# Gelu's tanh on up to six W1 items at once: attention, MLP and output projection in one kernel on one core

## The chip, the core and the metric

The kernel runs on one core of one Trainium2 chip. The metric is the device time of one execution in microseconds (us). The engines are named as in the profile: PE multiplies matrices, ACT (ScalarE) applies functions element by element, DVE (VectorE) does the other elementwise work, POOL (GpSimd) a few small things, and SP issues the DMAs.

## What is computed

The input x has 2048 rows of 1024 elements. It is normalized once; the normalized rows feed an attention of 32 heads (head size 32) and an MLP of width 3584, and the two results are multiplied:

```python
xn = _layernorm(x, axis=-1)
s = _A_ref(xn, A_wqkv, A_wo)                       # attention: softmax(q k^T / sqrt(32)) v, then wo
g = _silu(_B_ref(xn, B_w1, B_b1, B_w2, B_b2))
return x + s * g

def _B_ref(x, w1, b1, w2, b2):
    y = _layernorm(x, axis=-1)
    h = _gelu(jnp.einsum("bsd,df->bsf", y, w1) + b1)
    return jnp.einsum("bsf,fd->bsd", h, w2) + b2
```

The gelu is the approximation by tanh: with u = x (1 + 0.044715 x^2), it is x (1 + tanh(0.798 u)) / 2; the factor 1/2 is applied later. All tensors are bf16.

## The kernel before

**Attention.** The 32 heads are taken in eight groups of four. For each group (w in the code, 0 to 7) there are eight query blocks of 256 rows, and for each of those eight key pairs of 256 keys. One such unit (`unit`, L830) has a score matmul on PE (L846), which writes two pairs of PSUM banks, and two exponentials on ACT (L855), each 128 x 1024, which write P tiles in SBUF. Six PSUM banks hold three such pairs, so PE can be at most three exponentials ahead of ACT. PV matmuls (L612) multiply P with V; the row sums of P go through a tree of additions on DVE (`tree`, L877, with L872 and L886) and a matmul with ones. There are 512 units, and so some 1024 exponentials.

**Dense work.** Everything else on PE is called dense: the projections to Q, K and V (L683, L699, recorded at the helper's line 617), the MLP, and at the end the output projection. A dense item takes one of two PSUM banks (6 and 7) and is evicted by DVE.

**MLP.** The rows go through in eight chunks c of 256 rows (NCH = 8). Each chunk has 14 W1 items (NW1 = 14, `w1_item`, L1013): an item computes 256 of the 3584 hidden columns for 256 rows, that is 512 elements per partition, and DVE adds the bias and writes it to slot p % 20 of the ring hT (L1023; p = 14 c + pi, NH = 20 slots). Then four W2 items (`w2_item`, L1045) each read all 14 items of the chunk. A slot of the ring is free for a new W1 item when the four W2 items of its chunk have read it. `seq_mlp` (L1079) sets the order: between the W2 items of chunk c stand the first six W1 items of chunk c + 1, the other eight follow after the fourth.

**Gelu.** It runs in place on groups of neighbouring items in the ring, mostly four (L1027 to L1042): square (L1037), times 0.044715 plus 1 (L1038), times x (L1039), tanh on ACT (L1040), plus 1 (L1041), times x (L1042). The first three and the last two are on DVE. The scratch u is one of two buffers `ut_t[0]` and `ut_t[1]` of 2048 elements per partition, taken in turn (`geg`). In even chunks the groups are 4, 4, 4, 2 items, in odd ones 2, 4, 4, 4, and in the last chunk 2, 4, 4, 2, 2.

**What sets the order.** The kernel does not run loops on the chip: `_Plan` (L33) is a list scheduler in Python that simulates all engines with a cost for each operation (`c_b16`, `c_acts` and so on, L559 to L575), picks for each engine the next operation, and `emit` writes each engine's list with semaphore waits. Dependencies come from tokens such as ("h", slot) and ("ut", buffer). On DVE and ACT `pick` (L149) takes the ready operation with the lowest priority number: evictions and exponentials 0, quotients 1, gelu on DVE 3, trees 3.2, tanh 1. Some that have waited long are raised: DVE operations of priority 3 to 3.5 after 4000 ns, and ACT operations after 2500 ns, which then go ahead of the exponentials. PE takes scores first, as soon as a bank pair is free; a dense chunk is not started when it would leave ACT dry (`guard`). A W2 item is passed over until every DVE operation that its operands depend on has started (L302); PE then takes the head of another dense list. A change of one operation can so reorder everything that comes after it. In one stretch (the third of 30 us) the planner also adds a small pseudo-random term to positions and priorities, computed from the operations' numbers (`nz`, L83).

Of the kernel before, what the change touches and what calls it, by code (L numbers as in the profile page):

```python
# [6 lines left out]
ACT = mybir.ActivationFunctionType  # L7
ALU = mybir.AluOpType
BF16 = mybir.dt.bfloat16
F32 = mybir.dt.float32  # L10
I32 = mybir.dt.int32
# [21 lines left out]
class _Plan:  # L33
# [14 lines left out]
    def add(self, eng, fn, occ, lat, R=(), W=(), prio=3, item=None, sem=None, nbytes=0, rate=180.0, extra=()):  # L48
        o = _Op()
        o.eng, o.fn, o.occ, o.lat, o.prio = eng, fn, occ, lat, prio  # L50
        o.item, o.sem, o.nbytes, o.rate = item, sem, nbytes, rate
        o.idx = len(self.ops)
        o.users, o.ready, o.start, o.fin = [], 0.0, None, None
        o.dead, o.needs_inc, o.count, o.know = False, False, None, None
        o.l2, o.pas, o.exps = None, (), ()
        deps = {}
        for t in R:
            w = self.last_w.get(t)
            if w is not None:
                deps[w] = True  # L60
        for t in W:
            w = self.last_w.get(t)
            if w is not None:
                deps[w] = True
            for r in self.readers.get(t, ()):
                if r is not o:
                    deps.setdefault(r, False)
        for d in extra:
            deps[d] = True
        for t in R:  # L70
            self.readers.setdefault(t, []).append(o)
        for t in W:
            self.last_w[t] = o
            self.readers[t] = []
        deps.pop(o, None)
        o.deps = deps
        o.left = len(deps)
        for d in deps:
            d.users.append(o)
        self.ops.append(o)  # L80
        return o
# [379 lines left out]
def bass_recurrent_scan__mha_block__mixer_channel_mlp__prompt_kernel(  # L461
# [16 lines left out]
    NW1 = FB // 2  # L478
    EPS = 1e-5
    SCALE = 32 ** -0.5  # L480
    GC, GA = 0.7978845608028654, 0.044715
# [11 lines left out]
    with ExitStack() as st:  # L493
        def sb(name, shape, dt):
            return st.enter_context(nc.sbuf_tensor(name, list(shape), dt))
# [2 lines left out]
        o_d = nc.dram_tensor("o_scratch", (HG, 128, S), BF16).ap()  # L498

        NP, NPX, NPA, NH, NW1R, NW2R = 10, 16, 3, 20, 3, 4  # L500
        NTR, NWARM, NG0, AT = 4, 8, 3, 1
        ident = sb("ident", [128, 128], BF16)
        ones = sb("ones", [128, 32], BF16)
# [9 lines left out]
        hT = sb("hT", [128, NH, 2, 256], BF16)  # L513
# [3 lines left out]
        w2r = sb("w2r", [128, NW2R, 7, 256], BF16)  # L517
        b2b = sb("b2b", [128, D], BF16)
        b1T = sb("b1T", [128, FB], BF16)
        ut_t = [sb(f"ut{i}", [128, 4, 512], BF16) for i in range(2)]  # L520
        gw = sb("gw", [128, 4096], BF16)
        z_t = [gw[:, i * 1024:(i + 1) * 1024] for i in range(2)]
        zh_t = gw[:, 2048:4096].bitcast(F32)
# [21 lines left out]
        NXS = 10  # L545
        xst = [h_flat[:, i * 1024:(i + 1) * 1024] for i in range(NXS)]
        xnb = [gw[:, i * 1024:(i + 1) * 1024] for i in range(4)]
        iota_i = ut_t[0][:].rearrange("p a b -> p (a b)")[:, 0:256].bitcast(I32)

        def bank(i, lo=0, hi=512):  # L550
            return ps[:, i * 512 + lo:i * 512 + hi]
# [7 lines left out]
        def c_ps(n):  # L559
            return 77 + 1.0417 * n  # L560
# [4 lines left out]
        def c_b16(n):  # L565
            return 67 + 0.521 * n

        def c_b4(n):
            return 67 + 0.2605 * n
# [4 lines left out]
        def c_acts(n):  # L574
            return 82 + 0.8334 * n  # L575
# [3 lines left out]
        def linked(o, item):  # L579
            d = item.chunks[-1]  # L580
            if d not in o.deps:
                o.left += 1
                d.users.append(o)
            o.deps[d] = True
            item.evacs.append(o)

        def dve(fn, occ, R, W, prio, item=None, extra=()):
            o = add("DVE", fn, occ, DL, R, W, prio, extra=extra)
            if item is not None:
                linked(o, item)  # L590
            return o

        def act(fn, occ, R, W, prio, item=None):
            o = add("ACT", fn, occ, AL, R, W, prio)
            if item is not None:
                linked(o, item)
            return o
# [7 lines left out]
        def chunk(item, fn, occ, R, W=()):  # L605
            o = add("PE", lambda e, fn=fn, item=item: fn(e, item.bank), occ, TL, R, W, item=item)
            item.chunks.append(o)
            return o
# [7 lines left out]
        def mm(e, dst, lhsT, rhs, start, stop):  # L616
            return e.matmul(dst, lhsT=lhsT, rhs=rhs, start=start, stop=stop, skip_group_check=True)  # L617
# [4 lines left out]
        def fl3(t):  # L622
            return t[:].rearrange("p u j q -> p (u j q)")
# [140 lines left out]
        for n in range(NPR):  # L764
            groups = [(2 * n,), (2 * n + 1,)] if n < 2 else [(2 * n, 2 * n + 1)]
            for ts in groups:
                if ts == (AT,):
                    for k, f, sc in ((0, ACT.Copy, 1.0 / D), (1, ACT.Square, D ** -0.5)):
# [6 lines left out]
                                                         op1=ALU.subtract), 65,  # L775
# [209 lines left out]
        nw2, geg = {"n": 0}, {"n": 0}  # L985
# [16 lines left out]
        def make_y(c):  # L1002
            for t2 in range(2):
# [6 lines left out]
                dma(f"yt{t2}", lambda e, t2=t2: e.dma_start_transpose(yT[:, :, t2 * 128:(t2 + 1) * 128], yst_t[t2][:]),  # L1010
                    262144, [("yst", t2)], [("yT", t2)], occ=1300, rate=300.0, lat=2300)

        def w1_item(c, pi):  # L1013
            p = c * NW1 + pi
            gi, hs = p % NW1R, p % NH
            it = _Item("mlp")
            for f2 in range(2):
                for dc in range(DC):
                    def fn(e, b, f2=f2, dc=dc):
                        return mm(e, bank(b, f2 * 256, (f2 + 1) * 256), w1r[:, gi, dc, f2 * 128:f2 * 128 + 128], yT[:, dc, :],  # L1020
                                  dc == 0 and f2 == 0, dc == DC - 1)
                    chunk(it, fn, Q256, [("w1", gi), ("yT", 0), ("yT", 1)])
            w1_ev[p] = dve(lambda e: e.tensor_tensor(hT[:, hs], bank(it.bank).rearrange("p (k t) -> p k t", k=2),  # L1023
                                          b1T[:, 2 * pi:2 * pi + 2].unsqueeze(2).to_broadcast([128, 2, 256]), op=ALU.add),
                c_ps(512), [("b1",)], [("h", hs)], 0, it)
            half = c == NCH - 1 and pi in (NW1 - 3, NW1 - 1)
            if p % 4 != 3 and pi != NW1 - 1 and not (pi == 1 and c % 2) and not half:  # L1027
                return it
            k = 2 if (pi == NW1 - 1 and p % 4 != 3) or (pi == 1 and c % 2) or half else 4
            h0, n = hs - k + 1, k * 512  # L1030
            hs_ = [("h", h0 + i) for i in range(k)]
            ui = geg["n"] % 2
            geg["n"] += 1
            x_ = hT[:, h0:h0 + k].rearrange("p s k t -> p (s k t)")
            u_ = ut_t[ui][:].rearrange("p a b -> p (a b)")[:, 0:n]
            gp, ga = (1.4, -1) if c == NCH - 1 and pi >= 5 else (3, 1)
            dve(lambda e: e.tensor_tensor(u_, x_, x_, op=ALU.mult), c_b16(n), hs_, [("ut", ui)], gp)  # L1037
            dve(lambda e: e.tensor_scalar(u_, u_, GA, 1.0, op0=ALU.mult, op1=ALU.add), c_b4(n), [("ut", ui)], [("ut", ui)], gp)  # L1038
            dve(lambda e: e.tensor_tensor(u_, u_, x_, op=ALU.mult), c_b16(n), [("ut", ui)] + hs_, [("ut", ui)], gp)  # L1039
            act(lambda e: e.activation(u_, u_, ACT.Tanh, scale=GC), c_acts(n), [("ut", ui)], [("ut", ui)], ga)  # L1040
            dve(lambda e: e.tensor_scalar_add(u_, u_, 1.0), c_b4(n), [("ut", ui)], [("ut", ui)], gp)  # L1041
            dve(lambda e: e.tensor_tensor(x_, u_, x_, op=ALU.mult), c_b16(n), [("ut", ui)] + hs_, hs_, gp)  # L1042
            return it

        def w2_item(c, q):  # L1045
# [54 lines left out]
        def mlp(u0, u1):  # L1100
            seq = list(seq_mlp())
            cost = {"y": 0.0, "w1": 1.74, "w2": 6.1}
            total = sum(cost[s_[0]] for s_ in seq)
            at = 0.0
            for s_ in seq:
                pos = u0 + (u1 - u0) * at / total
                at += cost[s_[0]]
                if s_[0] == "y":
                    make_y(s_[1])
                    continue  # L1110
                if s_[0] == "w1":
                    load_w1(s_[1] * NW1 + s_[2])
                    it = w1_item(s_[1], s_[2])
                else:
                    for r in range(4):
                        w2slot[(s_[1], s_[2], r)] = load_w2(s_[2], r, [w1_ev[(4, 6, 8, 10)[r]]] if s_[1] + s_[2] == 0 else ())
                    it = w2_item(s_[1], s_[2])
                it.pos = pos
                (mq if s_[0] == "w1" else plan.dense["w2"]).append(it)
# [134 lines left out]
        for w in range(HG):  # L1254
# [24 lines left out]
            for qb in range(NQB):  # L1279
# [44 lines left out]
                for t2 in range(2):  # L1324
# [16 lines left out]
                    for nh in range(2):  # L1341
# [38 lines left out]
                        if fin and i2 == 3:  # L1380
                            hs_ = fl3(PR[0])[:, i2 * 512:(i2 + 1) * 512]
# [84 lines left out]
```

## Time and profile before

| | |
|---|---|
| median of 3 runs | 1036.16 us (1034.75 to 1036.66) |
| profiled execution | 1036.81 us |
| its span, first to last instruction | 1035.0 us |
| busy: ACT, PE, DVE | 98%, 96%, 92% |
| exponentials (L855) | 988 in the largest group, 923.6 us |
| tanh of gelu (L1040) | 33: 23 of 2048, 10 of 1024 elements per partition |
| dense MLP matmuls | 1792 for W1 (228.2 us busy), 1792 for W2 (223.7 us) |

The profile gives each group of instructions with its line, engine, operation, output and inputs, shape, number, busy time, mean duration, and the idle time of the engine before it with what ended it. Durations on one engine can overlap, so the mean duration is not the engine's time for one. The timeline gives starts and lengths in us; the table of stages gives, for a stretch, the busy time of PE, PE's weight loads, DVE, ACT and POOL, then PE's granted clock, the DMA share and GB/s. The granted clock was 0.997 over the span.

### The profile page before, as it was taken

Reading aid. Unit: us, or ns where it says so; the run is one execution under the profiler, and the core shown is the slowest. Engines: PE = TensorE matmul, PEld = TensorE weight load, DVE = VectorE, ACT = ScalarE, POOL = GpSimd, SP = SyncE. Lnnn points to the kernel's source line nnn. Section 1 sums busy time; section 2 is a strip of 40 time slices with the busy share of each in tenths; the row PEclk is TensorE's granted clock in tenths of the full one; section 3 lists DMA queues with packets and bytes.
Section 4 is the critical chain, followed back from the end, with each engine's and each line's share of the span. In section 5 each row is a group of like instructions: output and inputs, shape, how many; then the busy total and the mean of one; then the engine's idle time right before and its main releaser. Section 6 shows DMA issues by size and latency. Waiting matters only on the chain.

```text
span 1035.0 us, 31625 instructions
## 1 busy us (share of the span) xinstructions
PE 994.5 (96%) x14148; PEld 633.3 (61%) x14217; DVE 955.7 (92%) x1343; ACT 1015.9 (98%) x1093; POOL 12.2 (1%) x21
## 2 busy tenths in 40 slices
PE   8999999999999999999999999999999999999996
PEld 6656566666766566666665666666656665654433
DVE  7899999899799999997899999998999889978896
ACT  7999999999999999999999999999999999999996
POOL 2200000000000000000000000000000000000000
PEclk9999999999999999999999999999999999999998
DMA  7967756545766657446457575565365762963321
GB/s 204 171 155 212 192 151 188 166 114 153 205 182 143 177 163 221 120 133 190 136 147 196 149 224 164 149 181 160 84 165 161 208 177 70 294 209 121 121 84 53
DMA packets 318199, 167.99 MB, mean 162 GB/s; under 512 B 56688, under 2 KB 306032, under 8 KB 318064
## 3 DMA queue, kind: packets, MB, share of 16 engines
q1 hardware_dynamic: 318064, 165.98, 58.1%
q8 instruction: 111, 1.82, 0.7%
q14 instruction: 24, 0.20, 0.1%
HBM read 146.55 MB, written 12.06 MB: 153 GB/s over the span
## 4 chain that ended last, share of the span: by engine, by line
ACT 84%; PE 9%; DMA 3%; DVE 2%; issue 0%; SPq 0%; POOL 0%; DVEq 0%; another core or an unknown queue 0%
ACT P L855 78%; PE ps L617 6%; ACT ut L1040 4%; DMA w2r<-in_B_w_dram 2%; PE ps L846 2%; PE ps L612 1%; ACT gw L1067 1%; ACT P L1157 1%; DVE stats L785 1%; DMA xnT<-gw 0%; DMA hT<-in_A_x_dram 0%; DVE gw L748 0%; DVE PA L872 0%; DVE hT L1391 0%; ACT w2r L855 0%
## 5 line engine op out<-in xcount | busy, mean ns | idle before, releaser
L855 ACT ACTIVATE P<-ps 128x1024 bf16<-128x1024 f32 x988 | 923.6, 1238 | 2.9 <-PE ps L846 2.8
L872 DVE TENSOR_TENSOR PA<-P 128x2048 bf16<-128x2048 bf16 x173 | 209.5, 1215 | 33.5 <-ACT P L855 32.4
L617 PE MATMUL ps<-yT,w1r 128*128 128x256 bf16 x1792 | 228.2, 273 | 0.8 <-DVE QKT L702 0.5
L617 PE MATMUL ps<-w2r,hT 128*128 128x256 bf16 x1792 | 223.7, 273 | 4.0 <-DMA w2r<-in_B_w_dram 2.6
L846 PE MATMUL ps<-QKT 32*128 32x256 bf16 x4032 | 200.2, 273 | 12.9 <-ACT P L855 9.3
L886 DVE TENSOR_TENSOR PR<-PR,PA 128x2048 bf16<-128x2048 bf16 x173 | 209.4, 1211 | 1.3
L617 PEld LDWEIGHTS ps<-yT,w1r 128*128 128x128 bf16 x1792 | 163.6, 98 | 54.8 <-issue 30.2
L617 PEld LDWEIGHTS ps<-w2r,hT 128*128 128x128 bf16 x1792 | 163.3, 98 | 54.6 <-issue 30.8
L846 PEld LDWEIGHTS ps<-QKT 32*128 32x128 bf16 x4032 | 59.8, 92 | 142.1 <-ACT P L855 135.3
L612 PE MATMUL ps<-P,V 128*32 128x256 bf16 (+1 forms) x4080 | 136.8, 272 | 0.3 <-issue 0.3
L617 PE MATMUL ps<-xnT,wqk 128*128 128x512 bf16 (+1 forms) x507 | 118.7, 360 | 7.2 <-issue 2.0
L612 PEld LDWEIGHTS ps<-P,V 128*32 128x32 bf16 x4080 | 95.8, 96 | 31.3 <-issue 22.5
L617 PE MATMUL ps<-wv,xnT 128*128 128x256 bf16 (+1 forms) x575 | 85.8, 285 | 0.9 <-DVE QKT L702 0.7
L617 PEld LDWEIGHTS ps<-xnT,wqk 128*128 128x128 bf16 x560 | 49.3, 98 | 53.7 <-issue 15.6
L1023 DVE TENSOR_TENSOR hT<-ps,b1T 128x512 bf16<-128x512 f32 x112 | 76.4, 682 | 1.8 <-PE ps L617 1.1
L872 DVE TENSOR_TENSOR PR<-P 128x2048 bf16<-128x2048 bf16 x60 | 72.6, 1210 | 1.0 <-ACT P L855 0.8
L617 PEld LDWEIGHTS ps<-wv,xnT 128*128 128x128 bf16 x576 | 53.0, 98 | 22.2 <-issue 9.3
L1040 ACT ACTIVATE ut<-ut 128x2048 bf16<-128x2048 bf16 (+1 forms) x33 | 62.1, 1883 | 0.0
L941 DVE STREAM_TRANSPOSE nt<-ps 128x256 f32<-128x256 f32 x63 | 27.8, 442 | 14.9 <-PE ps L612 14.8
L702 DVE CAST QKT<-ps 128x512 bf16<-128x512 f32 x58 | 39.6, 683 | 1.8 <-PE ps L617 1.4
L1037 DVE TENSOR_TENSOR ut<-hT 128x2048 bf16<-128x2048 bf16 (+1 forms) x33 | 34.7, 1052 | 0.1
L1042 DVE TENSOR_TENSOR hT<-ut,hT 128x2048 bf16<-128x2048 bf16 (+1 forms) x33 | 34.6, 1050 | 0.0
(107 smaller groups left out, 581.3 us busy)
## 6 DMA issues: line engine op xcount, KB each, us to landing
w1r<-in_B_w_dram SPq DMA_DIRECT2D x112, 512.0 KB, 4.5
w2r<-in_B_w_dram SPq DMA_DIRECT2D x128, 448.0 KB, 4.6
hT<-in_A_x_dram SPq DMA_DIRECT2D x20, 256.0 KB, 3.8
wqk<-in_A_wqkv_dram SPq DMA_DIRECT2D x16, 256.0 KB, 4.3
yst<-in_A_x_dram SPq DMA_DIRECT2D x16, 256.0 KB, 4.7
g_scratch<-gw SPq DMA_DIRECT2D x32, 128.0 KB, 3.8
o_scratch<-ot SPq DMA_DIRECT2D x56, 64.0 KB, 3.6
xnT<-o_scratch SPq DMA_DIRECT2D x7, 512.0 KB, 7.2
```

What stands on the lines that cost most here:

```text
L612: ins = e.matmul(dst(j), lhsT=lhsT(j), rhs=rhs(j), start=start, stop=stop, tile_position=(0, 32 * j), skip_group_check=True)
L617: return e.matmul(dst, lhsT=lhsT, rhs=rhs, start=start, stop=stop, skip_group_check=True)
L702: dve(lambda e: e.tensor_copy(QKT[sl][:, which, tq * 512:(tq + 1) * 512], bank(it.bank)), c_ps(512), [], [(nm, sl, 2 * tq), (nm, sl, 2 * t ...
L846: ins = e.matmul(bank(b0[j], kk * 256, (kk + 1) * 256), lhsT=QKT[sl][32 * j:32 * j + 32, 1, kb * 128:(kb + 1) * 128], rhs=QKT[sl][32 * j:3 ...
L855: x = act(lambda e, h=h: e.activation(Pt[pi][:, 2 * h:2 * h + 2].rearrange("p j k q -> p (j k q)"), ps[:, pr[h] * 1024:(pr[h] + 1) * 1024] ...
L872: return dve(lambda e: e.tensor_tensor(dst[:].rearrange("p u j q -> p (u j) q"), src[:].rearrange("p u j k q -> p (u j) k q")[:, :, 0, :], ...
L886: return dve(lambda e: e.tensor_tensor(fl3(pr), fl3(pr), fl3(PA[i]), op=ALU.add), c_b16(2048), [("PA", i), tok], [tok], 3.2)
L941: dve(lambda e: e.transpose(nt_t[:], bank(pv.bank, 256, 512)), c_ps(256) + 120, [], [("nt",)], prio, pv)
L1023: w1_ev[p] = dve(lambda e: e.tensor_tensor(hT[:, hs], bank(it.bank).rearrange("p (k t) -> p k t", k=2), b1T[:, 2 * pi:2 * pi + 2].unsqueez ...
L1037: dve(lambda e: e.tensor_tensor(u_, x_, x_, op=ALU.mult), c_b16(n), hs_, [("ut", ui)], gp)
L1040: act(lambda e: e.activation(u_, u_, ACT.Tanh, scale=GC), c_acts(n), [("ut", ui)], [("ut", ui)], ga)
L1042: dve(lambda e: e.tensor_tensor(x_, u_, x_, op=ALU.mult), c_b16(n), [("ut", ui)] + hs_, hs_, gp)
```

## The change

The two scratch buffers become one tensor of eight items' width, with `ut_t[0]` and `ut_t[1]` as its halves. A table GRUNS, made ahead, says at which item a run ends and how long it is: up to six items (GMAX = 6), not across a chunk's end and not across the end of the ring; in the last chunk at most four, and two near its end. The DVE steps of a run are done in parts of at most four items, each part with its own half of the scratch tensor; a run of more than four starts with half 0 and puts the rest in half 1. One tanh then runs over all of the run's elements at once, up to 3072 per partition; it reads and writes both halves. Priorities and planner costs are as before.

```diff
+        GMAX = 6
-        ut_t = [sb(f"ut{i}", [128, 4, 512], BF16) for i in range(2)]
+        utw = sb("ut", [128, 8, 512], BF16)
+        ut_t = [utw[:, 4 * i:4 * i + 4] for i in range(2)]
...
+        GRUNS = {}
+        for c_ in range(NCH):
+            p_, end = c_ * NW1, (c_ + 1) * NW1
+            while p_ < end:
+                k_ = min(GMAX, end - p_, NH - p_ % NH)
+                if c_ == NCH - 1:
+                    k_ = min(k_, 2 if end - p_ <= 4 else 4)
+                GRUNS[p_ + k_ - 1] = k_
+                p_ += k_
...
-            half = c == NCH - 1 and pi in (NW1 - 3, NW1 - 1)
-            if p % 4 != 3 and pi != NW1 - 1 and not (pi == 1 and c % 2) and not half:
+            run = GRUNS.get(p)
+            if run is None:
                 return it
-            k = 2 if (pi == NW1 - 1 and p % 4 != 3) or (pi == 1 and c % 2) or half else 4
-            h0, n = hs - k + 1, k * 512
-            ui = geg["n"] % 2
-            geg["n"] += 1
+            hh = hs - run + 1
...
+            for h0 in range(hh, hh + run, 4):
+                k = min(4, hh + run - h0)
+                ui = 0 if h0 > hh or run > 4 else geg["n"] % 2
+                parts.append([h0, k, ui])
+            if run > 4:
+                parts[1][2] = 1
+                geg["n"] = 0
+            else:
+                geg["n"] += 1
...
+            for h0, k, ui in parts:
+                hs_ = [("h", h0 + i) for i in range(k)]
...
+                dve(lambda e, u_=u_, x_=x_: e.tensor_tensor(u_, x_, x_, op=ALU.mult), c_b16(n), hs_, [("ut", ui)], gp)
...
+            u0 = 4 * parts[0][2]
+            ua = utw[:, u0:u0 + run].rearrange("p a b -> p (a b)")
+            uts = [("ut", q_[2]) for q_ in parts]
+            act(lambda e: e.activation(ua, ua, ACT.Tanh, scale=GC), c_acts(run * 512), uts, uts, ga)
+            for x_, u_, n, hs_, ui in views:
+                dve(lambda e, u_=u_: e.tensor_scalar_add(u_, u_, 1.0), c_b4(n), [("ut", ui)], [("ut", ui)], gp)
+                dve(lambda e, u_=u_, x_=x_: e.tensor_tensor(x_, u_, x_, op=ALU.mult), c_b16(n), [("ut", ui)] + hs_, hs_, gp)
             return it
```

More of the change, by code (lines that the diff above doesn't have):

```diff
@@ L547, in bass_recurrent_scan__mha_block__mixer_channel_mlp__prompt_kernel @@
         xnb = [gw[:, i * 1024:(i + 1) * 1024] for i in range(4)]
-        iota_i = ut_t[0][:].rearrange("p a b -> p (a b)")[:, 0:256].bitcast(I32)
+        iota_i = utw[:].rearrange("p a b -> p (a b)")[:, 0:256].bitcast(I32)
         def bank(i, lo=0, hi=512):
@@ L1025, in w1_item @@
                 c_ps(512), [("b1",)], [("h", hs)], 0, it)
-            half = c == NCH - 1 and pi in (NW1 - 3, NW1 - 1)
-            if p % 4 != 3 and pi != NW1 - 1 and not (pi == 1 and c % 2) and not half:
-                return it
-            k = 2 if (pi == NW1 - 1 and p % 4 != 3) or (pi == 1 and c % 2) or half else 4
-            h0, n = hs - k + 1, k * 512
-            hs_ = [("h", h0 + i) for i in range(k)]
-            ui = geg["n"] % 2
-            geg["n"] += 1
-            x_ = hT[:, h0:h0 + k].rearrange("p s k t -> p (s k t)")
@@ L1035, in w1_item @@
-            u_ = ut_t[ui][:].rearrange("p a b -> p (a b)")[:, 0:n]
-            gp, ga = (1.4, -1) if c == NCH - 1 and pi >= 5 else (3, 1)
[L1037 to L1040, printed above, removed]
@@ L1041, in w1_item @@
-            dve(lambda e: e.tensor_scalar_add(u_, u_, 1.0), c_b4(n), [("ut", ui)], [("ut", ui)], gp)
-            dve(lambda e: e.tensor_tensor(x_, u_, x_, op=ALU.mult), c_b16(n), [("ut", ui)] + hs_, hs_, gp)
+            run = GRUNS.get(p)
+            if run is None:
+                return it
+            hh = hs - run + 1
+            gp, ga = (1.4, -1) if c == NCH - 1 and pi >= 5 else (3, 1)
+            parts = []
+            for h0 in range(hh, hh + run, 4):
+                k = min(4, hh + run - h0)
+                ui = 0 if h0 > hh or run > 4 else geg["n"] % 2
+                parts.append([h0, k, ui])
@@ new lines, in w1_item @@
+            if run > 4:
[3 more added lines that the diff above has]
+                geg["n"] += 1
+            views = []
+            for h0, k, ui in parts:
+                hs_ = [("h", h0 + i) for i in range(k)]
+                n = k * 512
+                x_ = hT[:, h0:h0 + k].rearrange("p s k t -> p (s k t)")
+                u_ = utw[:, 4 * ui:4 * ui + k].rearrange("p a b -> p (a b)")
+                views.append((x_, u_, n, hs_, ui))
+                dve(lambda e, u_=u_, x_=x_: e.tensor_tensor(u_, x_, x_, op=ALU.mult), c_b16(n), hs_, [("ut", ui)], gp)
+                dve(lambda e, u_=u_: e.tensor_scalar(u_, u_, GA, 1.0, op0=ALU.mult, op1=ALU.add), c_b4(n), [("ut", ui)], [("ut", ui)], gp)
+                dve(lambda e, u_=u_, x_=x_: e.tensor_tensor(u_, u_, x_, op=ALU.mult), c_b16(n), [("ut", ui)] + hs_, [("ut", ui)], gp)
```

## The prediction

> **What bounds the kernel now.** I read the page first: busy time, then the chain that ended last, then ScalarE's own groups with shapes kept apart.
>
> ```profile
> PE 994.5 (96%) x14148; PEld 633.3 (61%) x14217; DVE 955.7 (92%) x1343; ACT 1015.9 (98%) x1093; POOL 12.2 (1%) x21
> ...
> ACT 84%; PE 9%; DMA 3%; DVE 2%; issue 0%; SPq 0%; POOL 0%; DVEq 0%; another core or an unknown queue 0%
> ...
> L855 ACT ACTIVATE P<-ps 128x1024 bf16<-128x1024 f32 x988 | 923.6, 1238 | 2.9 <-PE ps L846 2.8
> ```
>
> ACT is busy 1015.9 of 1035.0 us and carries 84% of the chain, nearly all of it the exponentials of line 855. Its idle time is 19.1 us, and the slices of the page put it in the prologue and the tail: the view of waits gives it one wait of 4.6 us at the last activation, and from 60 to 1000 us the table of stages shows 90.00 of 90, 349.26 of 350, 424.36 of 425 and 75.00 of 75 us busy. So a saving on ACT is a saving in the end, as long as PE and DVE keep delivering. They have little room: PE is busy 72.63 of 75 us from 925 to 1000.
>
> Next, what one tanh costs ACT. The groups by shape:
>
> ```profile
> L1040 ACT ACTIVATE ut<-ut 128x2048 bf16<-128x2048 bf16 x23 | 49.2, 2140 | 0.0
> ...
> L1040 ACT ACTIVATE ut<-ut 128x1024 bf16<-128x1024 bf16 x10 | 12.9, 1290 | 0.0
> ...
> L653 ACT ACT_TABLE_LOAD x1 | 1.3, 1283 | 0.7 <-PEq L1451 0.7
> ```
>
> There is one table load in the whole execution, so going from Exp to Tanh and back loads nothing, and fewer tanh do not save loads. The means (2140 and 1290 ns) are durations, and durations overlap on ACT: the next instruction starts before the last one has ended. What an instruction takes from its engine is the distance to the next start, read in the timeline (start, length, engine, line):
>
> ```profile
> 426.52 2.15 ACT L1040 ACTIVATE ut<-ut 128x2048 bf16<-128x2048 bf16 x1
> 428.32 18.68 ACT L855 ACTIVATE P<-ps 128x1024 bf16<-128x1024 f32 x20
> ...
> 355.86 1.33 ACT L1040 ACTIVATE ut<-ut 128x1024 bf16<-128x1024 bf16 x1
> 356.81 17.80 ACT L855 ACTIVATE P<-ps 128x1024 bf16<-128x1024 f32 x19
> ```
>
> 2048 elements: 428.32 - 426.52 = 1.80 us. 1024 elements: 0.95 (starts over the trace give 0.947). So 1024 more elements cost 0.853, and the fixed part is 0.947 - 0.853 = 0.094 us.
>
> **Part 1, fewer tanh.** Before: 33 (23 of 2048, 10 of 1024). After, from the rule in GRUNS with 14 items a chunk, a ring of 20 slots and runs of at most 6 that do not cross the ring's end: chunks 0 to 3 and 6 give 6, 6, 2; chunk 4 gives 4, 6, 4; chunk 5 gives 6, 4, 4; chunk 7 gives 2, 4, 4, 2, 2 as before. That is 26: twelve of 3072, six of 2048, eight of 1024. The elements are the same (112 items), so ACT saves 7 x 0.094 = **0.66 us**. A tanh of 3072 is not in the trace; I take 0.094 + 3 x 0.853 = 2.65 us. While it runs, exponentials wait: three score pairs are then full in PSUM, and PE goes on with MLP and projection matmuls, as it does today for 1.80 us, so I cost that wait at nothing.
>
> **Part 2, more small DVE instructions.** A run of six is done as 4 + 2 on DVE, five instructions each. Chunks 0 to 3 and 6 go from 4 groups to 5, the others keep their number: 25 more DVE instructions. By starts, a 2048 tensor_tensor takes 1.136 us and a 1024 one 0.602, so a split costs 2 x 0.602 - 1.136 = 0.067 us; 25 of them are 1.7 us more on an engine with 79 us idle. On no chain of 84% ACT; I take 0.
>
> **Part 3, the wait that is added.** Two separate buffers let a group start while the one before it was in its tanh. A run of six takes both. The last pair of items of chunks 0 to 3 and 6 must now wait until the first four of the run before it are multiplied out. Only after that pair's own five steps may W2 of the chunk start, since its items wait for all gelu steps. Today, in chunk 0 (L1023 is the W1 eviction, L1037 a group's first step, L1042 its last):
>
> ```profile
> 108.43 0.68 DVE L1023 TENSOR_TENSOR hT<-ps,b1T 128x512 bf16<-128x512 f32 x1
> ...
> 119.30 0.68 DVE L1023 TENSOR_TENSOR hT<-ps,b1T 128x512 bf16<-128x512 f32 x1
> ...
> 124.84 0.68 DVE L1037 TENSOR_TENSOR ut<-hT 128x1024 bf16<-128x1024 bf16 x1
> ...
> 138.64 1.21 DVE L1042 TENSOR_TENSOR hT<-ut,hT 128x2048 bf16<-128x2048 bf16 x1
> ...
> 148.72 0.68 DVE L1042 TENSOR_TENSOR hT<-ut,hT 128x1024 bf16<-128x1024 bf16 x1
> ```
>
> The pair's first step (124.84) stands 14 us ahead of the four's last one (138.64), and the first W2 matmul starts at 148.96, directly behind 148.72. With the shared buffer the pair starts at 139.8 (138.64 + 1.14), 15 us later, and W2 at about 164. The same reading elsewhere: chunk 2, the four end at 356.4 where the pair starts at 339.9 now, 16.5 later; chunk 6, 775.7 against 773.1, 2.6 later. Chunks 1 and 3 end in a four now: item 11's eviction plus today's latency of a closing group (219.2 + 18.0 and 422.1 + 19.3), then that group's own length, is 4 and 5 us later. Chunk 4's last four wait under 1 us by that reading; 5 and 7 keep their two buffers. Together W2 starts some **43 us** later, in five places.
>
> Does that cost time? Behind the waiting DVE instruction stand the instructions that the planner puts there, and it knows of the wait, so the queue is filled with others. None of the changed steps issues a DMA. On PE the W2 item is passed over and projections, the next chunk's W1 and attention run. The price is what PE lacks when these run out. Today's longest waits end at 365.9 and 580.3:
>
> ```profile
> 355.00:360.00 5.00, 5.00 (x51) 3.50 (x51) 5.00 (x7) 5.00 (x7) 0.00 (x0) 1.00 0.47 135
> 360.00:365.00 5.00, 3.92 (x68) 1.70 (x70) 5.00 (x8) 5.00 (x6) 0.00 (x0) 1.00 0.68 188
> ...
> 570.00:575.00 5.00, 4.30 (x87) 2.21 (x76) 5.00 (x6) 5.00 (x7) 0.00 (x0) 1.00 0.39 113
> ```
>
> PE (second column) falls to 3.92 and 4.30 of 5 us near their ends, and at chunk 0's end (145 to 150) it was still on projections. Bounds: nothing, if projections or W1 fill every added us; by the rate of those two rows against the 4.9 around them, 0.8 us in 5, the 43 us lose 43 x 0.16 = 6.9 us of PE; and if PE had nothing but attention, the share of line 617 in the span (about 656 of 1035, 63%) makes it 27 us. The last needs five waits with no dense work at all, which none of today's has, and I leave it out of the range. PE hands lost time on only at the end, where 925 to 1000 has 2.4 us idle that could take some of it up. I take 0: chunk 0's wait has projections at its end, and chunk 2's runs into 367, where the next head group's projections open.
>
> [...]
>
> **Sum.** The profiled execution took 1036.81 us (span 1035.0, 1.8 around it). 1036.81 - 0.66 + 0 + 0 = 1036.15. The runs shown have a median of 1036.16, 0.65 lower, so on their scale the saving alone is 1035.5; I keep 1036.1, since every unknown but the reordering can only add. A difference under 0.2% (2.1 us) is about what a measurement of this kernel can't tell from none.
>
> **Rivals.**
> - **A, the forecast:** ACT saves 0.66 us and W2's later start is filled. 1034.5 to 1038.2, about 1036.1. Chance 0.42.
> - **B, W2 late, PE behind (slower):** the 6.9 us less the 2.4 idle near the end: 1036.8 - 0.7 + 6.9 - 2.4 = 1040.6, up to 1043 if the 2.4 can't be used. It decides where projections are used up more than some 4 us before the pair's last multiply in chunks 0 and 2. For it: 360 to 365 us. Against it: 145 to 150. Chance 0.27.
> - **C, new holes in ACT (slower):** the order of all instructions is laid anew behind item 3 of chunk 0, and longer tanh and more DVE steps make PE late with scores, as at 176.5 us now (0.71 us). Four more: 1036.2 + 2.8 = 1039.0. Against it: only two holes over 0.6 us between 60 and 1000 us. Chance 0.11.
> - **D, holes go (faster):** the new order loses today's holes at 176 and 918 us (0.71 + 0.64) and a little of the 4.6 us wait at the end, say 1: 1036.2 - 2.3 = 1033.9. Chance 0.14.
> - **E, a tanh's fixed cost is its duration's (faster):** 2 x 1290 - 2140 = 440 ns, seven times 3.1 us: 1033.7. Against it, the starts above: 94 ns. Chance 0.06. The Trainium skill, ScalarE: Activation LUTs, "Rules for kernel authors", budgets about 0.3 us for an ACTIVATE beside 0.83 ns an element, which would make it 2.1 us and 1034.7; by the timeline its 0.83 holds (0.853 us for 1024) and its 0.3 is a duration's.
>
> **How the numbers follow.** Faster by over 0.2% is D and E, 0.20; within it A, 0.42; slower B and C, 0.38. The range runs from E's 1033.7 to B's upper 1043.0 and leaves out about 2 in 10; A's own is 1034.5 to 1038.2.
>
> **What would show it.** 26 tanh in line order, 2.65 us from a 3072 tanh to the next start, ACT's busy time 0.7 us lower. The pair's first step directly behind the four's last multiply, and W2 of chunk 0 near 164 us. For A: PE stays near 4.9 of 5 us before W2 starts and the last exponential ends about 0.7 us earlier. For B: PE idle over 1 us in several such stretches, W2 of the last chunk ending well after 924 us, and output projection left over behind the last exponential. I am wrong if ACT has new waits on line 846, or if a 3072 tanh takes more than its elements say.

## The result, and the profile after

| | before | changed |
|---|---|---|
| first comparison: median | 1036.78 us | 1033.99 us |
| ratio, 95% interval | | 0.9977 (0.9966 to 0.9987): 2.4 us faster, 1.3 to 3.5 |
| compared again (`control`, below) | 1035.59 us | 1033.99 us |
| ratio, 95% interval | | 0.9985 (0.9976 to 0.9994): 1.6 us faster, 0.6 to 2.5 |
| profiled execution: span, time | 1035.0, 1036.81 us | 1033.8, 1035.59 us |

One of the changed kernel's eight runs in the first comparison, 1227.88 us at a granted clock of 0.753, is not counted. The two comparisons together say about 1.9 us, just under the line of 0.2% (2.1 us). The forecast was 1036.1 us, with a range from 1033.7 to 1043.0. The measured 1033.99 lies in that range, but below the 1034.5 to 1038.2 of rival A, the forecast proper: the sign of the sum was right and its size too small.

The changed kernel's page, the same three lines as were read of before (lines of the code have moved: 855 is now 857, 1023 is 1035, the gelu steps are 1060 to 1069):

```profile
PE 1004.7 (97%) x14233; PEld 636.1 (62%) x14233; DVE 959.8 (93%) x1368; ACT 1015.4 (98%) x1086; POOL 11.9 (1%) x21
...
ACT 85%; PE 10%; DVE 3%; DMA 2%; issue 0%; SPq 0%; POOL 0%
...
L857 ACT ACTIVATE P<-ps 128x1024 bf16<-128x1024 f32 x988 | 920.7, 1234 | 1.8 <-PE ps L848 1.7
```

ACT still sets the end. It runs 7 instructions fewer (1086 for 1093), DVE 25 more (1368 for 1343), as counted ahead. PE's higher figure says nothing: 85 of its matmuls are missing from the trace of before (14148 records for 14233). The tanh by shape, and one of them in the timeline:

```profile
L1066 ACT ACTIVATE ut<-ut 128x3072 bf16<-128x3072 bf16 x12 | 35.9, 2996 | 0.0
...
L1066 ACT ACTIVATE ut<-ut 128x2048 bf16<-128x2048 bf16 x6 | 12.6, 2094 | 0.0
L1066 ACT ACTIVATE ut<-ut 128x1024 bf16<-128x1024 bf16 x8 | 10.0, 1253 | 0.0
```

```profile
128.31 2.88 ACT L1066 ACTIVATE ut<-ut 128x3072 bf16<-128x3072 bf16 x1
130.96 19.48 ACT L857 ACTIVATE P<-ps 128x1024 bf16<-128x1024 f32 x21
```

12, 6 and 8, and from start to start 130.96 - 128.31 = 2.65 us, where the mean duration is 3.00. All 26 add up to 50.24 us of ACT's time by starts, the 33 of before to 50.88: 0.64 us less, for 0.66 forecast.

Where is the rest? I took every start on ACT and set off what each instruction needs by itself (0.904 us for an exponential, tanh by length, 0.947 for a SiLU tanh). What is left is waiting. Two executions of each program:

| us | before | before_2 | changed | control |
|---|---|---|---|---|
| start of the first exponential | 12.7 | 12.7 | 13.3 | 13.0 |
| waiting from there to 60 us | 3.4 | 2.9 | 3.5 | 3.4 |
| waiting from 60 to 1000 us | 13.0 | 12.7 | 12.3 | 11.35 |
| end of the last exponential | 1025.1 | 1024.2 | 1024.3 | 1023.0 |
| from there to the end | 9.95 | 9.55 | 9.5 | 8.2 |
| span | 1035.0 | 1033.7 | 1033.8 | 1031.2 |

One program's two executions differ by 1.3 and 2.6 us, in the start, in the middle and in the tail, so one profile of each would not do. What repeats for one program and is missing in the other is the question of the experiments.

### The profile page after: what moved, and what is told of

Read it like the earlier page. It is cut to its first block, busy times and chain, and to the rows that moved or that the text cites. A ratio compares the mean times of both kernels' runs of the same rounds, so it can differ in the third digit from the quotient of the medians.

```text
span 1033.8 us, 31747 instructions
## 1 busy us (share of the span) xinstructions
PE 1004.7 (97%) x14233; PEld 636.1 (62%) x14233; DVE 959.8 (93%) x1368; ACT 1015.4 (98%) x1086; POOL 11.9 (1%) x21
## 4 chain that ended last, share of the span: by engine, by line
ACT 85%; PE 10%; DVE 3%; DMA 2%; issue 0%; SPq 0%; POOL 0%
ACT P L857 77%; PE ps L619 7%; ACT ut L1066 4%; PE ps L848 2%; ACT gw L1094 1%; PE ps L614 1%; ACT P L1184 1%; DMA w2r<-in_B_w_dram 1%; DMA yst<-in_A_x_dram 1%; ACT w2r L857 1%; DVE stats L787 1%; DMA hT<-in_A_x_dram 0%; DMA xnT<-gw 0%; DVE hT L1035 0%; DVE gw L750 0%
## 5 line engine op out<-in xcount | busy, mean ns | idle before, releaser
L848 PE MATMUL ps<-QKT 32*128 32x256 bf16 x4032 | 200.2, 273 | 11.3 <-ACT P L857 9.7
L619 PE MATMUL ps<-xnT,wqk 128*128 128x512 bf16 (+1 forms) x560 | 131.0, 362 | 3.3 <-DVE yst L1009 1.5
L1066 ACT ACTIVATE ut<-ut 128x3072 bf16<-128x3072 bf16 (+2 forms) x26 | 58.5, 2251 | 0.0
L1060 DVE TENSOR_TENSOR ut<-hT 128x1024 bf16<-128x1024 bf16 (+1 forms) x38 | 35.5, 934 | 0.2
L1062 DVE TENSOR_TENSOR ut<-ut,hT 128x1024 bf16<-128x1024 bf16 (+1 forms) x38 | 35.2, 925 | 0.0
```

Source lines behind the costliest of these rows:

```text
L848: ins = e.matmul(bank(b0[j], kk * 256, (kk + 1) * 256), lhsT=QKT[sl][32 * j:32 * j + 32, 1, kb * 128:(kb + 1) * 128], rhs=QKT[sl][32 * j:3 ...
L1060: dve(lambda e, u_=u_, x_=x_: e.tensor_tensor(u_, x_, x_, op=ALU.mult), c_b16(n), hs_, [("ut", ui)], gp)
L1062: dve(lambda e, u_=u_, x_=x_: e.tensor_tensor(u_, u_, x_, op=ALU.mult), c_b16(n), [("ut", ui)] + hs_, [("ut", ui)], gp)
L1066: act(lambda e: e.activation(ua, ua, ACT.Tanh, scale=GC), c_acts(run * 512), uts, uts, ga)
```

## The experiments

The theories. **Fixed cost:** each tanh taken off ACT is worth 0.094 us, 0.66 in all. **Duration:** each is worth 0.44 us, 3.1 in all. **Order:** the planner's new order is worth something by itself, because it loses stalls of the old one. **Wait:** the closing pair's wait for the scratch costs PE time, which something else outweighs. Ratios are against the kernel before on the same chip, with 95% intervals; 0.001 is about 1.0 us.

**control**, the changed kernel again.

> The changed kernel once more, beside the kernel before, to narrow the difference. If only the 7 tanh taken off ScalarE count (7 x 0.094 us), the difference is 0.7 us; if the new order of the instructions is worth more than that, it stays near the 2.4 us first measured; if each tanh is worth the fixed part of its duration (7 x 0.44 us), 3.1 us.

Measured 0.9985 (0.9976 to 0.9994), 1.6 us. Of the three expected values 3.1 us is outside the interval; 0.7 is just inside, 2.4 too. (The first comparison's interval has 3.1 and 2.4 in it, but not 0.7.)

**split2048 and split512**, the changed order with tanh issued in pieces. The planner is told nothing of it, so every engine's order is the same:

```diff
-            act(lambda e: e.activation(ua, ua, ACT.Tanh, scale=GC), c_acts(run * 512), uts, uts, ga)
+            def tanhs(e):
+                for a in range(0, run * 512, 2048):      # split512: 512
+                    b = min(a + 2048, run * 512)
+                    ins = e.activation(ua[:, a:b], ua[:, a:b], ACT.Tanh, scale=GC)
+                return ins
+            act(tanhs, c_acts(run * 512), uts, uts, ga)
```

> The changed kernel's order, instruction for instruction, with each tanh of 3072 issued as one of 2048 and one of 1024: 38 tanh, 12 more. Fixed cost by starts: 1.1 us over the changed kernel (12 x 0.094). Fixed cost by durations: 5.3 us over it. If ScalarE has slack in the order, nothing. Against the kernel before: with the order worth nothing it is 0.5 us slower (5 more tanh); if the order carries the gain it stays 1 to 2 us faster.

> The same order with every tanh issued in pieces of 512 elements: 112 tanh, 86 more than in the changed kernel. Fixed cost by starts: 86 x 0.094 = 8.1 us over it. By durations: 38 us. If ScalarE has slack behind a tanh, well under 8.

Measured: split2048 1035.45 us, 0.9997 (0.9987 to 1.0007), 1.5 us over `control` by the medians and 1.2 by the ratios, for 1.1 expected; split512 1042.18 us, 1.0061 (1.0045 to 1.0078), 8.2 us over it (7.9 by the ratios) for 8.1 expected. In split512's groups by shape:

```profile
L1069 ACT ACTIVATE ut<-ut 128x512 bf16<-128x512 bf16 x112 | 65.9, 834 | 0.0
```

A piece of 512 has a mean duration of 834 ns and takes 520 from start to start; all 112 take 58.24 us by starts, 8.0 more than the 26. The 8.2 us for 86 more instructions are 0.095 us each (0.092 by the ratios): the fixed cost is settled, the duration theory has fallen, and ACT has little slack that would take an instruction for nothing. The Trainium skill, Perfetto Trace Analysis, "Optimizing Scalar/DVE Operations", gives about 93 ns for Scalar on SBUF and says that the profiled latency is about twice that; the runs agree with the 93 by 94 and 95 ns, but not with the twice: by the mean durations the fixed part is 440 ns.

Against the kernel before, split2048 is 0.3 us faster (1.3 faster to 0.7 slower), between the two expected values: 0.5 slower if the new order is worth nothing, 1 to 2 faster if the order carries the gain. Its 5 more tanh and split512's 79 more cost 0.47 and 7.4 us, so the new order by itself comes out at 0.8 and 1.1 us faster, each with an uncertainty of a microsecond or more.

**gmax4 and gmax7**, the changed kernel with `GMAX = 4` (33 tanh) and `GMAX = 7` (23).

> The changed kernel with runs of at most four: 33 tanh again, in the new grouping (4, 2, 4, 4 where the kernel before has 2, 4, 4, 4). If the number of tanh is the gain, 0.66 us slower than the changed kernel; if the order is, anything, and then it should not lie 0.66 above it but show it in holes of ScalarE.

> The changed kernel with runs of up to seven items: 23 tanh, 3 fewer. By the fixed cost 0.3 us faster than the changed kernel; by durations 1.3 us. Longer runs also make later W2 items and longer stretches without an exponential (3.1 us): if these cost, it is slower than the changed kernel.

Measured: gmax4 0.9991 (0.9981 to 1.0001), gmax7 0.9978 (0.9969 to 0.9986). From 33 to 26 to 23 tanh the ratio falls from 0.9991 to 0.9981 (the middle of the two comparisons) and 0.9978: steps of 1.0 and 0.3 us where the fixed cost gives 0.66 and 0.28. The direction fits, but the intervals are wider than the steps, and each kernel has an order of its own. gmax7 is the fastest beside the changed kernel, not distinguishable from it. gmax4 has 33 tanh and is still 0.9 us faster than before (2.0 faster to 0.1 slower): by the point value that is order, not number.

**pairown and before_wait**, the wait by itself. In pairown the closing pair uses scratch items 6 and 7, free in a run of six; in before_wait the old kernel's closing pair shares the buffer of the four ahead of it, with all 33 tanh:

```diff
 pairown
+            own = run == 2 and c < NCH - 1
...
+                if own:
+                    ui = 2
...
+                o_ = (0, 4, 6)[ui]
+                u_ = utw[:, o_:o_ + k].rearrange("p a b -> p (a b)")
 before_wait
+            late = k == 2 and pi == NW1 - 1 and c < NCH - 1
-            ui = geg["n"] % 2
-            geg["n"] += 1
+            ui = (geg["n"] - late) % 2
+            geg["n"] += not late
```

> The changed kernel, but the pair of items that closes a chunk works in scratch items 6 and 7, which a run of six leaves free, so that it no longer waits for the run ahead of it. If the later W2 is filled with other matmuls, as forecast, the time stays within 0.5 us of the changed kernel. If the wait costs matmul time, it is 1 us or more faster, with less idle time on PE ahead of the W2 items.

> The kernel before with one part of the change alone: in the even chunks the closing pair of items shares the scratch buffer of the four ahead of it and so waits for them; tanh stay 33. If the added wait costs matmul time (rival B), 1 us or more slower than before. If it is filled, as forecast, within 0.5 us. If a later W2 is what makes its weights arrive in time, 0.5 to 1 us faster, with less waiting of PE for w2r.

Measured: pairown 0.9990 (0.9980 to 1.0001), 0.5 us slower than `control` by the ratios and 1.25 by the medians, with W2 of chunk 0 starting at 145.1 instead of 158.1 us. Taking the wait away gains nothing. before_wait 1.0013 (1.0004 to 1.0022): 1.3 us slower than before (0.4 to 2.3), against `before_2` 0.9. Its W2 items start 7 to 14 us later in chunks 0 and 2 to 6. Both edits lay the order anew, so neither tries the wait alone, and before_wait's profile shows no place where it loses: its span is 1034.3 us, its waits for w2r 1.6. Whether the wait costs in the old grouping is open; in the new one nothing shows that it does.

**before_2**, the kernel before against itself.

> The kernel before against itself: the time should differ by nothing, and shows how finely two kernels can be told apart here. Its profile is the question: in the first profile PE waited 2.6 us for W2's weights (DMA w2r) and ScalarE had holes at 176 and 918 us behind those waits. If these belong to the order of the kernel before, they come again near the same places, 1 us or more in all; if they are accidents of one execution, there are none, or others.

Measured 1.0004 (0.9995 to 1.0013): half a microsecond is the noise of such a comparison. Its profile is the point. First the profile read ahead of the prediction, then before_2's; of each the timeline of PE, with W2 matmuls and the next scores, and that of ACT, with the exponentials:

```profile
175.42 0.72 PE L617 MATMUL ps<-w2r,hT 128*128 128x256 bf16 x5 [0.92 <-DMA w2r<-in_B_w_dram]
176.07 0.40 PE L846 MATMUL ps<-QKT 32*128 32x256 bf16 x8
```

```profile
173.62 2.20 ACT L855 ACTIVATE P<-ps 128x1024 bf16<-128x1024 f32 x2
176.52 1.94 ACT L855 ACTIVATE P<-ps 128x1024 bf16<-128x1024 f32 x2 [0.71 <-PE ps L846]
```

```profile
173.17 2.25 PE L617 MATMUL ps<-w2r,hT 128*128 128x256 bf16 x19 [0.75 <-DMA w2r<-in_B_w_dram]
175.35 0.40 PE L846 MATMUL ps<-QKT 32*128 32x256 bf16 x8
```

```profile
173.06 2.20 ACT L855 ACTIVATE P<-ps 128x1024 bf16<-128x1024 f32 x2
175.80 4.83 ACT L855 ACTIVATE P<-ps 128x1024 bf16<-128x1024 f32 x5 [0.54 <-PE ps L846]
```

The score matmuls (L846) stand behind the W2 matmuls in PE's list: while a W2 matmul waits for its weights they wait too, and ACT runs dry. By starts the hole is 1.10 us (176.52 less 173.62 and two exponentials of 0.904) and 0.93; a second at 917.6 and 916.7 us is 0.80 and 0.78. The loads before the first came in a bunch: two of them landed after 6.5 us in before_2 where the median is 4.5, and from 170 to 172 us the DMA share in its table of stages is 0.99. The sums over the view of waits, before, before_2, changed:

```profile
PE ps L617 <- DMA w2r<-in_B_w_dram: 2.6, 3, 0.9
```

```profile
PE ps L617 <- DMA w2r<-in_B_w_dram: 1.9, 3, 0.8
```

```profile
PE ps L619 <- DMA w2r<-in_B_w_dram: 0.5, 2, 0.3
```

`control` has no such line, and the changed kernel's timeline has no hole at either place. So these stalls come with the old order. (The 0.8 us hole at 101.8 us in the changed kernel's first profile does not come again in `control`: that one is an accident.) gmax7 has 1.5 us of such waits again, gmax4 1.7, before_wait 1.6; by starts ACT's holes in gmax7 are 0.55 and 0.89 us, and it is as fast as the changed kernel all the same. So the holes alone do not sort these kernels by time.

The tail has a second thing that repeats. The last matmuls of the last half unit, before, then before_2, then control:

```profile
1025.48 0.34 PE L612 MATMUL ps<-P,ones 128*32 128x128 bf16 x12
...
1027.04 0.24 PE L612 MATMUL ps<-P,ones 128*32 128x128 bf16 x4 [1.21 <-issue]
```

```profile
1024.57 0.34 PE L612 MATMUL ps<-P,ones 128*32 128x128 bf16 x12
1025.90 0.24 PE L612 MATMUL ps<-P,ones 128*32 128x128 bf16 x4 [0.99 <-issue]
```

```profile
1023.16 0.40 PE L614 MATMUL ps<-P,V 128*32 128x128 bf16 x16
1023.38 0.40 PE L614 MATMUL ps<-P,ones 128*32 128x128 bf16 x16
```

In the old program PE stops for 1.21 and 0.99 us ahead of its last four, for nothing that the profile shows, and everything after waits for these four. (In before_light, below, with the same order, the stop is there too, but 0.38 us.) The changed program has no stop there in `control`, and none in its other executions; it has one of 0.2 to 0.5 us 4 to 5 us earlier. In the old program's traces a 16 KB transfer of the instruction queue starts at 1024.34 and 1023.48 us and takes 1.2 and 1.0 us. It is over before the stop begins, and PE goes on 1.47 and 1.41 us after its end. In before_light, before_lat3600 and after_lat3600 that distance is 1.47, 1.31 and 1.39, though the stops last 0.38, 0.16 and 1.00 us: the end of the stop keeps its distance to the transfer, so PE is probably waiting for code. (The changed program's earlier stop ends 1.2 to 1.6 us after such a transfer, too.) That is argued from the times, not tried.

**before_light and after_light**, both orders with W2's loads cut to a seventh from the fifth on (stale weights, planner not told):

```diff
+            full = nw2["n"] <= NW2R
+            dst, src = (w2r[:, i], src) if full else (w2r[:, i, 0:1], src[:, 0:1])
-            dma(f"w2{i}", lambda e: e.dma_start(w2r[:, i], src), 458752, ...)
+            dma(f"w2{i}", lambda e: e.dma_start(dst, src), 458752, ...)
```

> The kernel before in its own order, but only the first four loads of W2's weights are whole; each later one brings one of its seven blocks (a seventh of the bytes), so the rest of the weights are stale and the output is not the reference's. If PE's waits for W2's weights (1.9 and 2.6 us in two profiles, ScalarE holes of 1.3 us and more in all at 176 and 917 us) are what the old order costs, they go and it is 0.7 to 1.3 us faster than the kernel before. If the holes come from something else, no change.

> The changed kernel in its own order with the same loads cut to a seventh (output not the reference's either). It has no such waits, so by the same theory it stays within 0.4 us of the changed kernel, and 0.66 us faster than the cut kernel before, the tanh alone. If the changed order is better in some other way, it stays 1.5 us or more ahead of the cut kernel before.

Measured: before_light 1.0001 (0.9990 to 1.0012), after_light 0.9989 (0.9978 to 1.0001). In before_light's trace the waits for w2r and both holes are gone, and ACT's waiting from 60 to 1000 us is 11.3 us instead of 13.0 and 12.7. That names the cause of the holes. But the time did not fall by 0.7 to 1.3 us: a miss. Its profile waits 4.4 us ahead of 60 us (3.4 and 2.9 before), where the loads are still the same, so the start hid it there; whether in all runs, their times can't say. The two cut kernels differ by 1.2 us, between the 0.66 of the tanh alone and the 1.5 of an order better in some other way. after_light was to stay within 0.4 us of the changed kernel; by the ratios of `control` and of the first comparison it is 0.4 and 1.2 us slower.

**before_lat3600 and after_lat3600**, both kernels with one planner number changed (`lat=3600.0` for `lat=3100.0` in `load_w2`): a new order each, tanh unchanged.

> The kernel before with one number of its planner changed: a load of W2's weights is taken to land 0.5 us later (3600 in place of 3100 ns). All 33 tanh stay, the order of the instructions after the first W2 is laid anew. If order alone is worth something through these waits, they shrink and it is 0.5 to 1 us faster than before; if the waits only move to other places, no change.

> The changed kernel with the same number of the planner changed. It has next to no such waits to lose: within 0.5 us of the changed kernel. If any new order is worth a microsecond either way, it will show here.

Measured: 0.9993 (0.9983 to 1.0004) and 0.9992 (0.9982 to 1.0001): the two are now alike. The new order costs the changed kernel 0.7 to 1.6 us by the ratios, and gains the old one 0.7 (0.4 lost to 1.8 gained). The waits for w2r did not go in before_lat3600 (2.0 us, holes at 264 and 916): a miss. What did change is the tail: before_lat3600 has a stop of 0.16 us ahead of its last eight matmuls, where before has one of 1.21 ahead of its last four, and after_lat3600 has one of 1.0 us ahead of its last eleven that the changed kernel has not. Where the stop is follows the order, whichever kernel it is; how long it is differs between executions as well.

**All profiles from one start.** ACT's first 76 instructions are the same, by name and shape, in all fourteen profiles; yet the 76th starts anywhere from 69.7 to 73.2 us. Taken from there to the end, the two orders can be compared without that scatter. The terms below are the tanh beyond 26 at 0.094 us, ACT's holes of over 0.4 us, and what the last eight groups of 16 matmuls take beyond 1.97 us (the stop, or the half clock of the last section):

| us | 76th starts | from there to the end | tanh | holes | last groups | what is left |
|---|---|---|---|---|---|---|
| before | 70.31 | 964.72 | 0.66 | 1.90 | 1.40 | 960.76 |
| before_2 | 69.76 | 963.95 | 0.66 | 1.71 | 1.18 | 960.40 |
| before_light | 71.33 | 961.86 | 0.66 | 0 | 0.56 | 960.64 |
| changed | 70.92 | 962.88 | 0 | 0.80 | 1.57 | 960.51 |
| control | 70.55 | 960.64 | 0 | 0 | 0 | 960.64 |
| after_light | 72.25 | 960.64 | 0 | 0 | 0 | 960.64 |
| split2048 | 72.44 | 961.66 | 1.13 | 0 | 0 | 960.53 |
| split512 | 73.18 | 968.88 | 8.08 | 0 | 1.43 | 959.37 |

Seven profiles of the two orders agree within 0.4 us once these terms are off, so in the traces they come through in full. split512 lies 1.2 us lower: ACT's other waits are shorter there by that much. In the six profiles of other orders 959.4 to 961.4 is left.

## Why the prediction was right or wrong

- **What bounds it:** right. ACT's busy time still sets the end, and 86 more instructions on it came out nearly in full, 8.2 us. But ACT was not without waits from 60 to 1000 us: durations overlap, so the stages show it busy but for 1.4 us, while by starts it waits 13.0.
- **Part 1, 0.66 us:** right, in the counts (26 tanh), the length (2.654 us by starts for 2.65) and the price.
- **Part 2, 25 DVE instructions at nothing:** counts right; nothing in the runs speaks against it, and no run tries it alone.
- **Part 3, W2 43 us later in five places:** wrong in size. W2 of chunk 0, forecast near 164 us, starts at 159.2. Between the first profiles, W2 of chunks 0 to 7 starts 10.2 and 7.7 us later, 5.4 earlier, 1.7 later, then 11.6, 5.5, 6.2 and 2.5 earlier, and the last W2 ends 8.8 earlier. Chunk 2 on DVE in the changed kernel (1069 is the last step, 1060 the first):

```profile
341.89 1.22 DVE L1069 TENSOR_TENSOR hT<-ut,hT 128x2048 bf16<-128x2048 bf16 x1
...
348.03 0.68 DVE L1060 TENSOR_TENSOR ut<-hT 128x1024 bf16<-128x1024 bf16 x1
...
360.50 0.68 DVE L1069 TENSOR_TENSOR hT<-ut,hT 128x1024 bf16<-128x1024 bf16 x1
```

  The pair does wait for the run's first four, as said. But I let the four of the new run end when the old group of four did (356.4), and they end at 343: four of the six items start on DVE before the run's last item is there (317.5, with the last evicted at 324.8). And I gave the pair its old 25 us, of which it takes 13, with fewer gelu groups side by side. Nothing speaks against its price of 0: pairown gains nothing, though its order is another one. For the old grouping before_wait leaves it open.
- **The sum's zero for a new order:** this is the step that failed. The forecast kept 1036.1, "since every unknown but the reordering can only add", and the reordering took away. Rival D had named it, with the same two holes, at 0.14, and gave 1033.9 us. The holes of 176 and 918 us went, 1.7 to 1.9 us of ACT's time by starts in two profiles of before, for the 1.35 that D read from idle times. D's second half, 1 us of the tail, came by a stop of PE's (1.0 to 1.2 us, 0.4 in before_light) that the forecast did not have: the view of waits had it only as idle time by "issue". That D's sum is so near is partly luck: it leaves out the 0.66 us of the tanh, and the changed kernel's own accidents and its later start (below) take some of the gain back.
- **Rival E** gave 1033.7, nearly the measured time, by a mechanism that has fallen. The time alone could not have told D from E; split512 did.
- **What stays open:** the terms of the order and the tanh add up to some 3.5 us, and from ACT's 76th instruction to the end the two profiles of before are 3.2 us longer on average than the changed, control, after_light and split2048 ones (the last without its 12 tanh). The timed runs say 1.9. What may make up the difference lies ahead of that start: it comes at 69.8 to 71.3 us in the old order's three profiles and at 70.6 to 73.2 in the new order's five, though ACT's list is the same up to there; whether that is chance was not tried. Nor do the timed runs of before_light confirm the W2 stalls: by them the stalls are worth 0, at most some 1 us. The tail's stop is measured in the traces only. Shifting PE's code by a few instructions would show whether the stop is code that comes late; it was not tried.

## What to carry to other kernels

Price an instruction of a saturated engine by the distance between starts, not by its duration (0.094 for 0.44 us here), and try it by issuing the same work in more pieces within the same order. Where a planner lays the whole order anew, profile both programs twice, and compare them from an instruction up to which they are the same: stalls that come back at the same place belong to the order, and can outweigh the change itself. When a step is made to wait for another, work out when the other will end after the change, not when its predecessor ends now.

## What the runs showed of the hardware that was not expected

PE's granted clock can fall to half in the tail of one execution and not of another, of the same program. Stages of 1 or 2 us, changed kernel, then control (the last three columns are the clock, the DMA share and GB/s):

```profile
1024.00:1025.00 1.00, 1.00 (x49) 1.00 (x44) 1.00 (x3) 0.30 (x1) 0.00 (x0) 0.50 0.00 0
1025.00:1026.00 1.00, 1.00 (x48) 1.00 (x43) 0.51 (x1) 0.00 (x0) 0.00 (x0) 0.50 0.21 72
```

```profile
1021.00:1023.00 2.00, 1.71 (x88) 1.32 (x92) 1.30 (x3) 1.98 (x3) 0.00 (x0) 1.00 0.33 125
1023.00:1024.00 1.00, 0.78 (x56) 0.60 (x44) 1.00 (x2) 0.00 (x0) 0.00 (x0) 1.00 0.00 0
```

The same eight groups of 16 matmuls, from the first start to the last end, take 3.55 us at 0.50 and 1.97 at 1.00, so 1.6 us of one profile's tail are the clock's. The clock is at half from 1023.25 us for 3.41 us; split512 and gmax4 have such a stretch at the same place, and no profile of the old order has one before its last half unit is done. The Trainium skill, TensorE: Matmul & The Clock Gate, "Part 1: The HAM clock gate", has the gate at half rate after an idle window of about 3.4 us, the window running free of the kernel. The half rate and the length agree, and a phase that differs between executions would fit; but PE was not idle here: it was busy 1.70 of the 3.41 us ahead of the drop (1.71 in split512, 1.56 in gmax4).
